# Two-head attention pairs on a padded array against four heads on 64x64 quarters, with the transposes moved to the DMA queue

## The chip, the cores and the metric

The kernel runs on one core of a Trainium2 chip. TensorE (PE) multiplies, VectorE (DVE), ScalarE (ACT) and GpSimd (POOL) work on the results, and DMA queues, most of them driven by SyncE (SP), move data. The metric is the time of one execution on the device in microseconds (us), as the median of a few runs; lower is better.

## The reference

Attention without a softmax, for 8 batches, 12 heads, 448 tokens and 64 values per head, followed by a gated two-layer network over the 3584 tokens:

```python
scores = scale * np.matmul(q, k.transpose(0, 1, 3, 2))     # scale = 1/8
attn = np.maximum(scores, 0.0) ** 2 / S                    # S = 448
x = np.matmul(attn, v)          # the 12 heads side by side: 3584 x 768
h = x @ w_in                                               # 768 x 2048
g = h * (1.0 / (1.0 + np.exp(-1.702 * h)))
out = g @ w_out                                            # 2048 x 768
```

The two constant factors of the attention are left out on the chip and folded into later scales (SC = 64 x 448 = 28672).

## The kernel before

Data arrive as float32, are cast to float16, multiplied, and accumulated in float32 in PSUM.

**Attention.** `attn_pair` handles two heads of one batch. The 448 tokens of a head lie on 112 partitions with four tokens each (`SQ` = 112). Five DMAs on SP's queue bring q, k and v (L64, L66, L69), VectorE casts them, and eight TensorE transposes against an identity (L82) put q and k with the head's 64 values on the partitions, the first head on partitions 0 to 63, the second on 64 to 127; VectorE copies the result to `qkt` (L89). For each of four groups of 112 keys, two matmuls with 64 rows each give the scores of the two heads (`sc`, L96), ScalarE takes the relu (`rl`, L103), VectorE squares it (`attnT`, L104), and two matmuls add to `av` (L106). There the stationary operand `vn` is 128 columns wide and holds v of one head beside 64 columns of zeros (POOL's memset, L71, VectorE's casts, L73), so that both heads' results land in their own half of one accumulator. ScalarE copies `av` to `xt` (L113). There are 48 such pairs.

**First layer.** `moe1_chunk` makes 128 of the 2048 hidden values for one batch of 448 tokens: six matmuls (L128), a sigmoid on ScalarE (L135) and a product on VectorE (L136). There are 16 of them per batch.

**Second layer.** `moe2_chunk` makes 128 tokens of the output from two batches' hidden values: two times 16 matmuls of 384 columns (L151), ScalarE's scaled copy (L157), and output DMAs on SP's queue (L165).

**Order.** Stage 0 is the first batch's attention, followed by the weights: 28 DMAs on SP's queue (L177, L182), each cast by VectorE. In stage 1 to 8, `weave` deals the next batch's attention pairs among the first layer's chunks of the batch before, and in every second stage among seven chunks of the second layer too. The tile framework makes the semaphores and orders each engine's instructions.

## Time and profile before

| what | value |
|---|---|
| time, median of 3 runs | 535.62 us (535.36 to 536.15) |
| span of the profiled execution | 528.7 us (its own time is not listed apart; 6.9 us lie between its span and the median) |
| PE busy (matmul) | 481.4 us, 91% |
| DVE busy | 294.0 us, 56% |
| ACT busy | 281.3 us, 53% |
| POOL busy | 48.3 us, 9% |
| DMA | 57.14 MB moved, mean 108 GB/s |

The span runs from the first to the last instruction of the profiled execution. Busy time counts an engine's own instructions. Matmuls are pipelined and their ends are modelled, so the step from one start to the next says more than a matmul's listed duration.

### The profile page before, as it was taken

The page shows a single profiled execution, that of the slowest core. Times are in us where ns is not written, and L with a number is a line of the kernel's source. Part 1 is how long each engine was busy: PE and PEld are TensorE (multiplying, and loading weights), DVE is VectorE, ACT ScalarE, POOL GpSimd, SP SyncE. Part 2 cuts the span into 40 slices and gives each one's busy share as a digit, 9 for nine tenths or more (in the row PEclk, how much of TensorE's full clock was granted, in tenths as well). Part 3 has the DMA queues.
Part 4 walks back from the last instruction along what each step waited for, and adds up shares of the span by engine and source line. Part 5 has one row for each costly group of instructions (what it writes and reads, how often), then busy time and mean ns, then how long its engine had stood idle before and what let it go on. Part 6 is the DMA issues. An engine that isn't in the chain of part 4 may idle for free.

```text
span 528.7 us, 7760 instructions
## 1 busy us (share of the span) xinstructions
PE 481.4 (91%) x2816; PEld 237.0 (45%) x2816; DVE 294.0 (56%) x589; ACT 281.3 (53%) x426; POOL 48.3 (9%) x54
## 2 busy tenths in 40 slices
PE   1776838789999999999999999999999999999996
PEld 1332413334455554444456554444456554445663
DVE  3686857887730248887740248887740248855000
ACT  2566415776741447776741447776741457764111
POOL 1121001211100001011110000111010000100000
PEclk9889977999999999999999999999999999999999
DMA  6668888563232434443332434443332432000222
GB/s 166 168 227 263 268 256 184 139 147 97 71 102 64 109 95 104 105 100 88 77 100 60 113 94 105 106 102 80 80 100 62 112 96 69 2 1 0 61 71 79
DMA packets 109158, 57.14 MB, mean 108 GB/s; under 512 B 91200, under 2 KB 101952, under 8 KB 109120
## 3 DMA queue, kind: packets, MB, share of 16 engines
q1 hardware_dynamic: 109120, 56.64, 40.6%
q8 instruction: 22, 0.36, 0.3%
q14 instruction: 16, 0.13, 0.1%
HBM read 45.61 MB, written 11.01 MB: 107 GB/s over the span
## 4 chain that ended last, share of the span: by engine, by line
PE 68%; DVE 10%; DMA 9%; ACT 4%; issue 4%; POOL 3%; SPq 2%; DVEq 0%; POOLq 0%; ACTq 0%
PE op L151 26%; PE ht L128 17%; PE av L106 15%; PE sc L96 8%; ACT rl L103 3%; DMA t<-in_moe_w_in_dram 3%; POOL vn L71 3%; DVE qkt L89 2%; DMA t<-in_moe_w_out_dram 2%; PE qkt_ps L82 2%; DVE vn L73 2%; DVE gt L136 2%; DMA kn<-in_k_dram 2%; DMA vs<-in_v_dram 2%; DVE attnT L104 1%
## 5 line engine op out<-in xcount | busy, mean ns | idle before, releaser
L103 ACT ACTIVATE rl<-sc 112x896 f16<-112x896 f32 x192 | 166.1, 921 | 49.2 <-PE sc L96 48.6
L128 PE MATMUL ht<-xt,win 128*128 128x448 f16 x768 | 176.3, 353 | 6.4 <-DVE gt L136 3.5
L151 PE MATMUL op<-wout,gt 128*128 128x384 f16 x896 | 151.8, 326 | 0.0
L104 DVE TENSOR_TENSOR attnT<-rl 112x896 f16<-112x896 f16 x192 | 119.0, 624 | 41.8 <-ACT rl L103 39.0
L106 PE MATMUL av<-attnT,vn 112*128 112x448 f16 x384 | 107.8, 364 | 7.7 <-DVE attnT L104 7.4
L151 PEld LDWEIGHTS <-gt 128*128 128x128 f16 x896 | 86.8, 98 | 60.4 <-issue 3.2
L128 PEld LDWEIGHTS <-win 128*128 128x128 f16 x768 | 70.7, 97 | 82.2 <-issue 22.4
L135 ACT ACTIVATE sg<-ht 128x448 f32<-128x448 f32 x128 | 70.0, 549 | 50.5 <-PE ht L128 46.4
L136 DVE TENSOR_TENSOR gt<-ht,sg 128x448 f16<-128x448 f32 x128 | 79.1, 619 | 19.5 <-ACT sg L135 19.1
L71 POOL MEMSET vn<- 112x1024 f16 x48 | 47.8, 995 | 407.9 <-PE av L106 392.4
L157 ACT ACTIVATE osb<-op 128x384 f32<-128x384 f32 x56 | 27.5, 491 | 105.4 <-PE op L151 105.4
L96 PE MATMUL sc<-qkt 64*112 64x448 f16 x384 | 69.0, 388 | 11.2 <-ACT rl L103 5.6
L76 DVE CAST qnf<-qn 112x512 f16<-112x512 f32 x48 | 24.4, 509 | 96.8 <-PE qkt_ps L82 89.1
L106 PEld LDWEIGHTS <-vn 112*128 112x128 f16 x384 | 33.6, 99 | 47.9 <-issue 35.5
L96 PEld LDWEIGHTS <-qkt 64*112 64x112 f16 x384 | 24.9, 127 | 65.6 <-issue 40.9
L113 ACT ACTIVATE xt<-av 128x448 f16<-128x448 f32 x48 | 26.1, 544 | 37.2 <-PE av L106 35.4
L82 PE MATMUL qkt_ps<-identf,qnf 112*128 112x112 f16 x192 | 20.6, 223 | 16.6 <-DVE identf L53 9.3
L73 DVE CAST vn<-vs 112x256 f16<-112x256 f32 x96 | 23.6, 286 | 20.9 <-POOL vn L71 20.0
L89 DVE COPY qkt<-qkt_ps 128x896 f16<-128x896 f16 x48 | 29.6, 616 | 2.8 <-PE qkt_ps L82 2.8
L82 PEld LDWEIGHTS <-qnf 112*128 112x128 f16 x192 | 16.0, 103 | 28.3 <-DVE qnf L76 13.4
L78 DVE CAST knf<-kn 112x512 f16<-112x512 f32 x48 | 22.5, 470 | 2.1 <-DMA kn<-in_k_dram 2.1
L82 PE MATMUL qkt_ps<-identf,knf 112*128 112x112 f16 x192 | 19.9, 224 | 0.4 <-DVE knf L78 0.4
(12 smaller groups left out, 34.5 us busy)
## 6 DMA issues: line engine op xcount, KB each, us to landing
qn<-in_q_dram SPq DMA_DIRECT2D x96, 112.0 KB, 3.1
kn<-in_k_dram SPq DMA_DIRECT2D x96, 112.0 KB, 3.1
vs<-in_v_dram SPq DMA_DIRECT2D x48, 224.0 KB, 2.9
t<-in_moe_w_in_dram SPq DMA_DIRECT2D x12, 512.0 KB, 4.5
t<-in_moe_w_out_dram SPq DMA_DIRECT2D x16, 384.0 KB, 3.8
out_dram<-osb SPq DMA_DIRECT2D x8, 336.0 KB, 3.1
out_dram<-osb SPq DMA_DIRECT2D x8, 288.0 KB, 2.6
out_dram<-osb SPq DMA_DIRECT2D x8, 240.0 KB, 2.6
```

Source lines behind the costliest of these rows:

```text
L71: nc.gpsimd.memset(vn, 0.0)
L73: nc.vector.tensor_copy(out=vn[:, h, :, h * D:(h + 1) * D], in_=vs[:, h, :, :])
L82: nc.tensor.matmul(out=qkt_ps[:, i, si * SQ:(si + 1) * SQ], lhsT=src[:, si, :, :], rhs=identf[:, :], is_transpose=True,)
L89: nc.vector.tensor_copy(out=qkt, in_=qkt_ps[:, :, 0:S])
L96: nc.tensor.matmul(out=sc[0:SQ, h, 0:S], lhsT=qkt[64 * h:64 * h + 64, 1, t2 * SQ:(t2 + 1) * SQ], rhs=qkt[64 * h:64 * h + 64, 0, 0:S], star ...
L103: nc.scalar.activation(out=rl, in_=sc[0:SQ, :, 0:S], func=AF.Relu)
L104: nc.vector.tensor_tensor(out=attnT[:, t2, :, :], in0=rl, in1=rl, op=ALU.mult)
L106: nc.tensor.matmul(out=av[:, 0:S], lhsT=vn[:, h, t2, :], rhs=attnT[:, t2, h, :], start=(t2 == 0 and h == 0), stop=(t2 == 3 and h == 1),)
L128: nc.tensor.matmul(out=ht[:, 0:S], lhsT=win[:, kk, f * 128:(f + 1) * 128], rhs=xt[:, kk, :], start=(kk == 0), stop=(kk == NK - 1),)
L135: nc.scalar.activation(out=sg, in_=ht[:, 0:S], func=AF.Sigmoid, scale=1.702 / SC)
L136: nc.vector.tensor_tensor(out=gt[:, f, boff:boff + S], in0=ht[:, 0:S], in1=sg, op=ALU.mult)
L151: nc.tensor.matmul(out=op[:, 0:NOUT], lhsT=gt[:, f, jm:jm + 128], rhs=wout[:, f, n * NOUT:(n + 1) * NOUT], start=(f == 0), stop=(f == NF - 1),
```

## The change

- **Heads.** A unit is four heads of one batch: heads 2pr and 2pr+1 on partitions 0 to 63, heads 6+2pr and 7+2pr on 64 to 127. A token index is p*7 + j, with p from 0 to 63 and j from 0 to 6 (`J` = 7). There are 3 units per batch (`NP`), 24 in all (`NU`), and 7 slots (j) in each.
- **Loads.** Six DMAs per unit on SP's queue, each of 64 partitions with two rows of 1792 bytes.
- **Casts and transposes.** VectorE casts q and k, POOL casts v; q and k are then transposed from SBUF to SBUF by `dma_start_transpose` on SP's queue, two transposes per unit, each of 128 x 896 float16 (seven blocks of 128 x 128). TensorE's transposes, the identity and the copy `qkt` are gone, and so are the zero-padded `vn` and its memset.
- **Scores and av.** Per slot four score matmuls of 448 columns, each with 64 rows and 64 stationary columns, on the four quarters of the array; likewise four for `av`. ScalarE's relu and VectorE's square work on 128 x 896.
- **Copy of av.** VectorE copies `av` (128 x 896) to `xt`, in one or two pieces, once per unit.
- **First layer.** Tokens come in eight groups of 384 or 512 in turn (`gblk`). One ScalarE instruction gives the gated value (`Gelu_apprx_sigmoid`); POOL multiplies by SC and casts to float16.
- **Second layer.** VectorE makes the scaled copy; two output DMAs for each 128 tokens.
- **Weights.** Eight DMAs on POOL's queue, four each for `win` and `wout`, which cast from float32 to float16 on the way.
- **Order.** Written by hand (`manual_schedule`). A visit issues the scores of two new slots, the `av` matmuls of the slots before, and then the new slots' relu and square. The first batch's visits come first, then chunks of the two layers (`m1`, `m2`) with a visit after every 3.4 us that the program reckons for them; when a group of tokens needs a batch that is not done, visits are issued one behind the other until it is.

```diff
-    ident = cst.tile([SQ, SQ], F32)
-    make_identity(nc, ident)
...
+    win = [cst.tile([128, NK, WQ * 128], F16, name=f"win{i}") for i in range(NF // WQ)]
+    wout = [cst.tile([128, WQ, DM], F16, name=f"wout{i}") for i in range(NF // WQ)]
...
+    def load(u):
+        b, pr = divmod(u, NP)
+        st = {}
+        for n, t in (("k", k), ("q", q), ("v", v)):
+            x = stp.tile([128, 2, S], F32, name=f"{n}st", tag=f"{n}st")
+            for s in range(2):
+                h0 = 6 * s + 2 * pr
+                nc.sync.dma_start(
+                    out=x[64 * s:64 * s + 64, :, :],
+                    in_=t[b, h0:h0 + 2].rearrange("a (p j) d -> p a (j d)", j=J))
+            st[n] = x
+        units[u] = st
+    def cast(u):
+        st = units[u]
+        for n in ("k", "q"):
+            c = c16.tile([128, J, 2, D], F16, name=f"{n}16", tag=f"{n}16")
+            nc.vector.tensor_copy(
+                out=c.rearrange("p j a d -> p a j d"),
+                in_=st[n].rearrange("p a (j d) -> p a j d", d=D))
+            st[n + "16"] = c
+        vv = v16p.tile([128, 2, J, D], F16, name="v16", tag="v16")
+        nc.gpsimd.tensor_copy(out=vv, in_=st["v"].rearrange("p a (j d) -> p a j d", d=D))
+        st["v16"] = vv
+    def trans(u):
+        st = units[u]
+        for n in ("k", "q"):
+            t = qkT.tile([128, J, 128], F16, name=f"{n}T", tag=f"{n}T")
+            nc.sync.dma_start_transpose(
+                out=t[:, :, :], in_=st[n + "16"].rearrange("p j a d -> p (j a d)"))
+            st[n + "T"] = t
+    def scores(u, j):
+        st = units[u]
+        sc = ps_s.tile([128, 2, 512], F32, name="sc", tag="sc")
+        for s in range(2):
+            for a in range(2):
+                r = slice(64 * a, 64 * a + 64)
+                c = slice(64 * s, 64 * s + 64)
+                nc.tensor.matmul(
+                    out=sc[c, a, 0:S],
+                    lhsT=st["kT"][r, j, c],
+                    rhs=st["qT"][r, :, c],
+                    start=True, stop=True)
+        return sc
+    def relu2(u, j, sc):
+        rl = rlp.tile([128, 2, S], F16, name="rl", tag="rl")
+        nc.scalar.activation(out=rl, in_=sc[:, :, 0:S], func=AF.Relu)
+        at = atp.tile([128, 2, S], F16, name="at", tag="at")
+        nc.vector.tensor_tensor(out=at, in0=rl, in1=rl, op=ALU.mult)
+        return at
+    def av_mm(u, j, at):
+        st = units[u]
+        if j == 0:
+            st["av"] = ps_v.tile([128, 2, 512], F32, name="av", tag="av")
+        for s in range(2):
+            for a in range(2):
+                r = slice(64 * s, 64 * s + 64)
+                nc.tensor.matmul(
+                    out=st["av"][64 * a:64 * a + 64, s, 0:S],
+                    lhsT=st["v16"][r, a, j, :],
+                    rhs=at[r, a, :],
+                    start=(j == 0), stop=(j == J - 1))
+    def xt_evac(u):
+        b, pr = divmod(u, NP)
+        av = units[u]["av"]
+        lo = b * J
+        while lo < (b + 1) * J:
+            g = max(i for i in range(NG) if gcum[i] <= lo)
+            hi = min((b + 1) * J, gcum[g + 1])
+            if g not in xts:
+                xts[g] = xtp.tile([128, 2, NP, 512], F16, name="xt", tag="xt")
+            nc.vector.tensor_copy(
+                out=xts[g][:, :, pr, 64 * (lo - gcum[g]):64 * (hi - gcum[g])],
+                in_=av[:, :, 64 * (lo - b * J):64 * (hi - b * J)])
+            lo = hi
+        units[u] = None
+    slots = [(u, j) for u in range(NU) for j in range(J)]
+    pend = []
+    pos = [0]
+    done_units = [0]
+    def visit(n):
+        new = slots[pos[0]:pos[0] + n]
+        pos[0] += len(new)
+        scs = [scores(u, j) for u, j in new]
+        ready = []
+        while pend:
+            ready.append(pend.pop(0))
+            if ready[-1][1] == J - 1:
+                break
+        for u, j, at in ready:
+            av_mm(u, j, at)
+        if ready and ready[-1][1] == J - 1:
+            xt_evac(ready[-1][0])
+            done_units[0] = ready[-1][0] + 1
+        for (u, j), sc in zip(new, scs):
+            pend.append((u, j, relu2(u, j, sc)))
...
-        sg = mo.tile([128, S], F32, tag="sg")
-        nc.scalar.activation(out=sg, in_=ht[:, 0:S], func=AF.Sigmoid, scale=1.702 / SC)
-        nc.vector.tensor_tensor(out=gt[:, f, boff:boff + S], in0=ht[:, 0:S], in1=sg,
-                                op=ALU.mult)
...
+                out=ht[:, 0:n], lhsT=w[:, kk, fo:fo + 128],
+                rhs=xts[g][:, kk // NP, kk % NP, 0:n],
+                start=(kk == 0), stop=(kk == NK - 1))
+        gf = gfp.tile([128, 512], F32, name="gf", tag="gf")
+        nc.scalar.activation(out=gf[:, 0:n], in_=ht[:, 0:n],
+                             func=AF.Gelu_apprx_sigmoid, scale=1.0 / SC)
+        nc.gpsimd.tensor_scalar(out=gts[g][:, f, 0:n], in0=gf[:, 0:n],
+                                scalar1=SC, scalar2=1.0, op0=ALU.mult, op1=ALU.mult)
+    osb = {}
+    def m2(g, m, h):
+        if h == 0:
+            osb[g, m] = osp.tile([128, DM], F32, name="osb", tag="osb")
+        ot = osb[g, m]
+        op = ps_m.tile([128, 512], F32, name="op", tag="mm")
+        for f in range(NF):
+            nc.tensor.matmul(
+                out=op[:, 0:NOUT],
+                lhsT=gts[g][:, f, m * 128:(m + 1) * 128],
+                rhs=wout[f // WQ][:, f % WQ, h * NOUT:(h + 1) * NOUT],
+                start=(f == 0), stop=(f == NF - 1))
+        nc.vector.tensor_scalar(out=ot[:, h * NOUT:(h + 1) * NOUT], in0=op[:, 0:NOUT],
+                                scalar1=1.0 / SC, scalar2=None, op0=ALU.mult)
+        if h == 1:
+            for i in range(2):
+                b, j = divmod(gcum[g] + 2 * m + i, J)
+                r0 = b * S + j
+                nc.sync.dma_start(out=out[r0:r0 + 63 * J + 1:J, :],
+                                  in_=ot[64 * i:64 * i + 64, :])
+    def w1(i):
+        nc.gpsimd.dma_start(
+            out=win[i],
+            in_=moe_w_in[:, i * WQ * 128:(i + 1) * WQ * 128].rearrange(
+                "(kk p) f -> p kk f", p=128))
+    def w2(i):
+        nc.gpsimd.dma_start(
+            out=wout[i],
+            in_=moe_w_out[i * WQ * 128:(i + 1) * WQ * 128, :].rearrange(
+                "(f p) d -> p f d", p=128))
+    def t1(g):
+        return 6 * (64 * gblk[g] / 2400.0 + 0.0025)
+    T2 = 16 * (NOUT / 2400.0 + 0.0025)
+    for ph in range(1, NG + 2):
+        a = [("m1", ph - 1, f) for f in range(NF)] if ph - 1 < NG else []
+        c = ([("m2", ph - 2, m, h) for m in range(gblk[ph - 2] // 2) for h in range(2)]
+             if ph >= 2 else [])
+        if a and c:
+            seq = []
+            ci = 0
+            for i, x in enumerate(a):
+                seq.append(x)
+                while ci < len(c) and (i + 1) * len(c) >= (ci + 1) * len(a):
+                    seq.append(c[ci])
+                    ci += 1
+            seq += c[ci:]
         else:
+            seq = a + c
+        moe += seq
+    with tc.manual_schedule():
+        loaded = [0]
+        prepped = [0]
+        def prefetch(upto_load, upto_prep):
+            while loaded[0] < min(NU, upto_load):
+                load(loaded[0])
+                loaded[0] += 1
+            while prepped[0] < min(NU, upto_prep):
+                cast(prepped[0])
+                trans(prepped[0])
+                prepped[0] += 1
+        prefetch(2, 0)
+        prefetch(2, 1)
+        prefetch(3, 2)
+        prefetch(3, 3)
+        for i in range(NF // WQ):
+            w1(i)
+        prefetch(6, 3)
+        for i in range(NF // WQ):
+            w2(i)
+        def step_visit(n):
+            u = slots[pos[0]][0]
+            prefetch(u + 4, u + 2)
+            visit(n)
+        while done_units[0] < NP:
+            if pos[0] < NP * J:
+                step_visit(min(2, NP * J - pos[0]))
+            else:
+                visit(0)
+        acc = 0.0
+        TV = 3.4
+        m1_done = 0
+        for it in moe:
+            if it[0] == "m1":
+                g = it[1]
+                need = NP * min(B, -(-gcum[g + 1] // J))
+                while done_units[0] < need:
+                    if pos[0] < len(slots):
+                        step_visit(2)
+                    else:
+                        visit(0)
+                m1(*it[1:])
+                acc += t1(g)
+            else:
+                m2(*it[1:])
+                acc += T2
+            if it[0] == "m1" and it[2] == NF - 1:
+                m1_done = it[1] + 1
+            if acc >= TV and (pos[0] < len(slots) or pend):
+                if pos[0] < len(slots):
+                    if slots[min(pos[0] + 1, len(slots) - 1)][0] // NP + 1 - 3 < m1_done:
+                        step_visit(2)
+                else:
+                    visit(0)
+                acc -= TV
```

## Rows read from the trace of the kernel before

**Rows 1.** The page's first lines: span, then each engine's busy time, share and instructions.

```profile
span 528.7 us, 7760 instructions
PE 481.4 (91%) x2816; PEld 237.0 (45%) x2816; DVE 294.0 (56%) x589; ACT 281.3 (53%) x426; POOL 48.3 (9%) x54
```

**Rows 2.** Busy time by stretch: length, busy us per engine, granted clock, DMA share, GB/s.

```profile
40.00:50.00 10.00, 6.95 (x41) 2.95 (x40) 8.02 (x15) 5.33 (x7) 0.95 (x1) 1.00 0.77 258
50.00:60.00 10.00, 7.07 (x37) 3.44 (x37) 7.26 (x13) 5.53 (x10) 1.20 (x1) 1.00 0.90 261
60.00:70.00 10.00, 8.80 (x46) 4.27 (x45) 7.25 (x15) 4.34 (x8) 0.00 (x0) 1.00 0.83 274
70.00:80.00 10.00, 1.83 (x12) 0.82 (x10) 5.59 (x13) 0.56 (x2) 0.00 (x0) 0.63 0.93 249
...
160.00:200.00 40.00, 39.77 (x250) 21.45 (x247) 12.23 (x26) 15.69 (x27) 1.90 (x2) 1.00 0.35 93
```

**Rows 3.** The chain that ended last, its final pieces: start us, us, what.

```profile
469.78 17.63 PE ht L128 x93
487.41 36.41 PE op L151 x224
```

**Rows 4.** Groups by line: shapes, count, busy us, mean ns, idle before.

```profile
L103 ACT ACTIVATE rl<-sc 112x896 f16<-112x896 f32 x192 | 166.1, 921 | 49.2 <-PE sc L96 48.6 <-DVE attnT L104 0.4 <-DVE qnf L76 0.2
L104 DVE TENSOR_TENSOR attnT<-rl 112x896 f16<-112x896 f16 x192 | 119.0, 624 | 41.8 <-ACT rl L103 39.0
L106 PE MATMUL av<-attnT,vn 112*128 112x448 f16 x384 | 107.8, 364 | 7.7 <-DVE attnT L104 7.4
L136 DVE TENSOR_TENSOR gt<-ht,sg 128x448 f16<-128x448 f32 x128 | 79.1, 619 | 19.5 <-ACT sg L135 19.1
L135 ACT ACTIVATE sg<-ht 128x448 f32<-128x448 f32 x128 | 70.0, 549 | 50.5 <-PE ht L128 46.4 <-DVE gt L136 4.1
L96 PE MATMUL sc<-qkt 64*112 64x448 f16 x384 | 69.0, 388 | 11.2 <-ACT rl L103 5.6 <-DVE qkt L89 4.0
L71 POOL MEMSET vn<- 112x1024 f16 x48 | 47.8, 995 | 407.9 <-PE av L106 392.4 <-DVE qkt L89 15.4
L157 ACT ACTIVATE osb<-op 128x384 f32<-128x384 f32 x56 | 27.5, 491 | 105.4 <-PE op L151 105.4
L82 PE MATMUL qkt_ps<-identf,qnf 112*128 112x112 f16 x192 | 20.6, 223 | 16.6 <-DVE identf L53 9.3 <-DVE qnf L76 7.4
```

**Rows 5.** Timeline of PE in the last attention stage: start us, us, instruction.

```profile
450.22 0.59 PE L96 MATMUL sc<-qkt 64*112 64x448 f16 x4
450.74 0.93 PE L128 MATMUL ht<-xt,win 128*128 128x448 f16 x4
451.63 0.40 PE L96 MATMUL sc<-qkt 64*112 64x448 f16 x2
451.96 0.36 PE L128 MATMUL ht<-xt,win 128*128 128x448 f16 x1
...
453.10 0.54 PE L106 MATMUL av<-attnT,vn 112*128 112x448 f16 x2
453.48 0.54 PE L128 MATMUL ht<-xt,win 128*128 128x448 f16 x2
...
455.90 0.36 PE L82 MATMUL qkt_ps<-identf,qnf 112*128 112x112 f16 x4
456.10 0.36 PE L82 MATMUL qkt_ps<-identf,knf 112*128 112x112 f16 x4
```

**Rows 6.** DMA issues on SP's queue by source: duration of the issue, then time to landing.

```profile
L69 SPq DMA_DIRECT2D vs<-in_v_dram x48: 318/340/614, 3.5 to 444.6; - x48
...
DMA to landing us min/median/max: 2.5/2.9/4.6
...
L165 SPq DMA_DIRECT2D out_dram<-osb x56: 314/412/589, 154.9 to 524.7; - x56
```

**Rows 7.** Timeline of the start: the first load's cast on VectorE.

```profile
5.08 0.43 DVE L76 CAST qnf<-qn 112x512 f16<-112x512 f32 x1 [5.08 <-DMA qn<-in_q_dram]
```

More of the change, by code (lines that the diff above doesn't have):

```diff
@@ L6 @@
 from concourse import bass_utils, mybir
-from concourse.masks import make_identity
 from concourse._compat import with_exitstack
@@ L36 @@
     SC = float(D * S)
-    cst = ctx.enter_context(tc.tile_pool(name="cst", bufs=1))
+    WQ = 4
+    gblk = [6, 8] * (B // 2)
+    gcum = [0]
+    for n in gblk:
+        gcum.append(gcum[-1] + n)
+    NG = len(gblk)
+    cst = ctx.enter_context(tc.tile_pool(name="cst", bufs=1))
+    stp = ctx.enter_context(tc.tile_pool(name="stp", bufs=3))
+    c16 = ctx.enter_context(tc.tile_pool(name="c16", bufs=2))
+    v16p = ctx.enter_context(tc.tile_pool(name="v16p", bufs=4))
+    qkT = ctx.enter_context(tc.tile_pool(name="qkT", bufs=3))
@@ L115, in attn_chunks @@
-    def attn_chunks(b):
-        xt = xtp.tile([128, NK, S], F16, name="xt", tag="xt")
-        xts[b] = xt
-        return [lambda hp=hp: attn_pair(b, hp) for hp in range(NHP)]
-    gts = {}
-    def moe1_chunk(b, f):
-        xt = xts[b]
-        gt = gts[b // 2]
-        boff = (b % 2) * S
-        ht = ps_m.tile([128, 512], F32, tag="mps")
+    osp = ctx.enter_context(tc.tile_pool(name="osp", bufs=3))
+    ps_s = ctx.enter_context(tc.tile_pool(name="ps_s", bufs=2, space=bass.MemoryType.PSUM))
@@ new lines @@
+    ps_v = ctx.enter_context(tc.tile_pool(name="ps_v", bufs=1, space=bass.MemoryType.PSUM))
+    ps_m = ctx.enter_context(tc.tile_pool(name="ps_m", bufs=2, space=bass.MemoryType.PSUM))
+    win = [cst.tile([128, NK, WQ * 128], F16, name=f"win{i}") for i in range(NF // WQ)]
+    wout = [cst.tile([128, WQ, DM], F16, name=f"wout{i}") for i in range(NF // WQ)]
+    units = {}
+    def load(u):
[10 more added lines that the diff above has]
+        units[u] = st
@@ L127, in moe1_chunk, with m1 @@
+    gts = {}
+    def m1(g, f):
+        n = 64 * gblk[g]
+        if f == 0:
+            gts[g] = gtp.tile([128, NF, 512], F16, name="gt", tag="gt")
+        ht = ps_m.tile([128, 512], F32, name="ht", tag="mm")
+        w = win[f // WQ]
+        fo = (f % WQ) * 128
         for kk in range(NK):
             nc.tensor.matmul(
-                out=ht[:, 0:S],
-                lhsT=win[:, kk, f * 128:(f + 1) * 128],
-                rhs=xt[:, kk, :],
-                start=(kk == 0), stop=(kk == NK - 1),
-            )
@@ L171, in moe2_chunks @@
-    def moe2_chunks(pair):
-        return [lambda m=m: moe2_chunk(pair, m) for m in range(2 * S // 128)]
-    def weight_chunks():
-        def w1(kk, hf):
-            t = tmp.tile([128, DFF // 2], F32, tag="wtmp")
-            nc.sync.dma_start(out=t, in_=moe_w_in[kk * 128:(kk + 1) * 128,
-                                                  hf * DFF // 2:(hf + 1) * DFF // 2])
-            nc.vector.tensor_copy(out=win[:, kk, hf * DFF // 2:(hf + 1) * DFF // 2], in_=t)
-        def w2(f):
-            t = tmp.tile([128, DM], F32, tag="wtmp")
-            nc.sync.dma_start(out=t, in_=moe_w_out[f * 128:(f + 1) * 128, :])
-            nc.vector.tensor_copy(out=wout[:, f, :], in_=t)
-        return ([lambda kk=kk, hf=hf: w1(kk, hf) for kk in range(NK) for hf in range(2)]
-                + [lambda f=f: w2(f) for f in range(NF)])
@@ L187, in weave @@
-    def weave(at, mc):
-        seq = []
-        ai = 0
-        for j, c in enumerate(mc):
-            while ai < len(at) and ai * len(mc) <= j * len(at):
-                seq.append(at[ai])
-                ai += 1
-            seq.append(c)
-        seq.extend(at[ai:])
-        return seq
-    for st in range(B + 1):
-        at = attn_chunks(st) if st < B else []
-        if st == 0:
-            seq = at + weight_chunks()
-        else:
-            mc = moe1_chunks(st - 1)
-            if st >= 2 and st % 2 == 0:
-                mc = mc + moe2_chunks(st // 2 - 1)
-            seq = weave(at, mc)
-        for c in seq:
-            c()
+                out=ht[:, 0:n], lhsT=w[:, kk, fo:fo + 128],
@@ new lines, in w1 @@
+    def w1(i):
[8 more added lines that the diff above has]
+                "(f p) d -> p f d", p=128))
+    moe = []
+    def t1(g):
+        return 6 * (64 * gblk[g] / 2400.0 + 0.0025)
+    T2 = 16 * (NOUT / 2400.0 + 0.0025)
```

102 lines of the change are left out of this document (6 added, 96 removed).

## The prediction

> **What bounds the kernel now.** I read the page's first lines, then the busy time by stretch, then the chain that ended last, then single instructions. PE is busy for 481.4 of 528.7 us, and no other engine for more than 294.0 [rows 1]. The stretches show two regimes. From stage 2 on PE is the limit: 39.77 of 40 us are busy at the full granted clock while the DMA engines are busy for a third [rows 2]. Up to about 80 us it is not: PE is busy for 7 to 9 of 10 us, and for 1.83 between 70 and 80 us, while the DMA engines are busy for 77 to 93% at 249 to 274 GB/s, 260 on average [rows 2]: there the weights and the next batch's heads arrive. So the change is worth what it takes off PE after the start, less what it adds to a start that DMA sets.
>
> **The two layers, which stay.** At the end 93 matmuls of 448 columns take 17.63 us, 0.190 each, and 224 of 384 columns take 36.41, 0.1625 each [rows 3]; between them lie 0.42 ns per column, so 512 columns take 0.217. The first layer has 768 matmuls, half of 384 columns and half of 512: 62.4 + 83.2 = 145.6 us. The second has 896 of 384: 145.6. Together 291.2, the same as before.
>
> **What leaves PE.** Scores are busy for 69.0 us, av for 107.8, transposes for 20.6 with q and about as much with k [rows 4]: some 218 us.
>
> **What replaces it.** A visit holds 8 score and 8 av matmuls of 448 columns on quarters. Two score matmuls on different rows (L96 x2) start at 451.63 and the next line at 451.96: 0.33 us for 0.19 of streaming, so they ran together and 0.14 went with the change from half rows to full [rows 5]. L96 x4 takes 0.52, two times 0.19 and 0.14. Four full matmuls in front of scores take 0.89, 0.13 over 0.76, and two av matmuls, which use the full array now, lead into other full ones after 0.38, nothing over [rows 5]. A visit is one block of quarters with one change in and one out, 0.27. If the four quarters run together it is 4 x 0.19 + 0.27 = 1.03; a weight load and its short matmul take 0.05 (four transposes from 455.90 to 456.10 [rows 5]), and 16 of those give 0.8 + 0.27 = 1.07. No row shows matmuls side by side in the columns: with two at a time the visit is 8 x 0.19 + 0.27 = 1.79, one at a time 3.3. I take 1.05, nearest to the rows that overlap already.
>
> Written out, the program has 12 visits in the first batch, 64 paced ones and a last one (4 of the paced in the first phase of the layers), and 10 issued one behind the other (8 of them at the second phase's start). Where nothing lies between visits, ScalarE sets the pace: two relus at 0.92 [rows 4], 1.84 a visit.
>
> **Engines that become no bound.** ScalarE: 168 relus at 0.92 and 128 gated values at 0.55: 225 us. VectorE: 168 squares at 0.62, 48 casts of 896 at 0.75 (0.43 for 512 [rows 7]), 24 copies of av at 1.24 (0.62 for 448 from PSUM), 56 output copies at 0.49 [rows 4]: 198 us. POOL: its memset does 1024 elements in 0.995 [rows 4], so 128 products of up to 512 and 24 casts of 896 are 86 us; a product would have to take 1.3 us, a first-layer chunk's PE time, to matter. All are priced at nothing under some 410 us of PE; should that cover be gone, each one's sum above is its cost. The gated value's second pass on VectorE (L136) and the memset go, also at no gain, since they are hidden now.
>
> **DMA and its queue.** SP issues six loads per unit; one like them costs it 0.34 us and lands after 2.9, an output DMA 0.41 [rows 6]. 144 loads and 56 outputs are 72 us. A transpose has no row. Below, it is a load of the same bytes, 0.34 us of queue; above, its seven blocks follow each other, each landing before the next, 7 x 2.9 = 20.3. I take 1 to 3 us, as one instruction of 229 KB with the bytes of a load: at 3 us SP's sum is 216 us, under PE. Behind a transpose, which waits for VectorE's cast, stand the later loads and outputs; three units of loads lie ahead, so these wait without PE. The Trainium skill (VectorE: DVE Perf Modes, The three transpose paths) gives 390 ns for a 128x128 transpose on TensorE and 1309 ns on the DMA crossbar. Seven of those in a row would be an estimated 9.2 us per transpose, and the sum would then be the fifth case's below instead of mine; no run here shows it.
>
> **The sum.** First scores: the first load is there at 5.08 us [rows 7], two casts make 6.6, two transposes with a landing of 2.9 about 10, and the 2.75 MB of two units take 10.6 us at 260 GB/s: I take 12 (10 to 14). First batch: 21 x 0.92 = 19.3, and 1.5 for its last square, av and copy: 32.8. First phase: 96 x 0.1625 = 15.6 and 4 x 1.05: 52.6. Eight visits at ScalarE's pace, 14.7: 67.3. Three chunks of 1.3 and a visit, then the first second-layer chunk: 72.3. It needs all of `wout`.
>
> Here stands the one new wait that I count. By then the queues have been given nine units (12.4 MB), both weights (12.6 MB read) and 2.75 MB of transposes: 27.7 MB, 107 us at 260 GB/s. The weights' last piece comes somewhat before the last unit: 100. Bounds: 85, as 274 GB/s came at a share of 0.83 [rows 2] and full use would be 330; and 148, if a casting DMA counts double for 12.6 MB. No DMA left POOL's queue before, so nothing shows its price. PE takes its instructions in order and waits 27.7 us; the forced visits' loads are late for the same reason, which is in the same 100. After it: 275.6 of the layers from the second phase on, 2 x 1.84 and 61 x 1.05: 343.4, less the 5.0 already counted. The end: 2 for the last chunk's gated value and product, and 4.9 from the last matmul to the end of the span, as now (523.8 to 528.7 [rows 1, 3]). 100 + 338.4 + 6.9 = 445.3 us of span. The median lies 6.9 above the span before (535.62 to 528.7), so 452.
>
> **The rivals.** Second: the weights are there sooner and the wait shrinks or goes, 424 to 437 us; for it, 3 KB and 2 KB rows in place of 256-byte ones, against it, 93% busy engines at 249 GB/s [rows 2]. Third: weights from POOL's queue are slow, doubled by the cast or late because POOL makes them behind its own work; `wout` at 148, 500 us. POOL's v casts and products stand behind these eight DMAs, so a blocked POOL holds the first layer's PSUM through ScalarE as well. The Trainium skill (SBUF — State Buffer, Who interferes with whom) says that VectorE's two-port casts lock POOL out while it writes descriptors; no row of before can show that. Fourth: only two quarters run together: 0.74 x 61 = 45 us more, 497. Fifth, the slower side: the transposes fill SP's queue. From the first transpose at 5 us to the last unit, then some 62 us of layers without attention and 5 at the end: 5 + 72 + 48 T + 67 passes 528.7 from T = 8.0 us on. At T = 10, 624 us of span, 631. For it, that the crossing lies inside the bounds of 0.34 and 20.3; against it, 229 KB that as a load occupy the queue for 0.34.
>
> **How the numbers follow.** The forecast case (437 to 470 us, 452 as its point) 0.47, earlier weights 0.10, slow weights 0.15, half-parallel quarters 0.14, transposes as the bound 0.14, of which 0.02 for a time within 0.2% of now. Runs of this kernel lie 0.15% apart, so 0.2% is about what can be told from no change. Faster is 0.47 + 0.10 + 0.15 + 0.14 = 0.86, slower 0.12. The range reaches from 418, under the second case's end by a first score at 10 us and visits at 1.0, to 510, over the third and fourth; it leaves out the fifth and what two mishaps together give.
>
> **What would show it.** Right: PE near 40 of 40 us from the second phase on; a visit of 16 quarter matmuls from first start to the next full one in about 1.05 us; PE's idle time before the first `op` matmul ended by the DMA into `wout` near 100 us; ScalarE without gaps in the first batch's relus; issues of transposes on SP under 3 us. Wrong: score matmuls released by transposes all along (fifth), visits near 1.8 (fourth), the first `op` after 130 us (third) or POOL's products pacing the first layer.

## The result, and the profile after

The changed kernel takes 461.49 us (median of 4 runs, 460.75 to 463.11), the kernel before 535.49 in the same comparison. The ratio on record is 0.865, 95% interval 0.8605 to 0.8695 (the two medians alone give 0.862, inside it). 452 was forecast. The profiled execution took 461.49 us itself, with a span of 459.7.

The page's head and two of its queues, after (answering to [rows 1]); a queue's line has packets, MB, and the share of 16 engines over the span:

```profile
span 459.7 us, 7621 instructions
PE 391.4 (85%) x3008; PEld 196.2 (43%) x3008; DVE 192.6 (42%) x308; ACT 212.0 (46%) x298; POOL 107.4 (23%) x164
...
q1 hardware_dynamic: 69760, 55.07, 54.9%
q0 software_dynamic: 5248, 6.29, 8.1%
```

PE is still the busiest engine, but its share fell from 91% to 85%: it lost 90.0 us of work, and the span only 69.0. PE's idle time rose from 47.3 to 68.3 us, and 54.4 of it lie before 120 us (65.6 us busy until then). Busy time by stretch, after, columns as in [rows 2]:

```profile
40.00:50.00 10.00, 7.68 (x44) 3.27 (x39) 4.19 (x7) 4.91 (x8) 1.73 (x5) 0.80 1.16 271
50.00:60.00 10.00, 0.00 (x0) 0.00 (x0) 0.00 (x0) 0.00 (x0) 1.35 (x2) 0.71 1.22 212
60.00:70.00 10.00, 0.00 (x0) 0.00 (x0) 0.00 (x0) 0.00 (x0) 0.00 (x0) 0.50 1.17 203
70.00:80.00 10.00, 9.07 (x59) 4.40 (x60) 2.50 (x4) 5.80 (x9) 2.14 (x5) 0.77 1.25 242
80.00:90.00 10.00, 9.24 (x87) 4.60 (x85) 4.41 (x7) 7.71 (x13) 4.71 (x9) 1.00 0.69 149
90.00:100.00 10.00, 6.71 (x64) 2.74 (x67) 8.88 (x13) 6.99 (x9) 2.76 (x3) 0.59 0.94 187
...
160.00:200.00 40.00, 40.00 (x339) 21.37 (x336) 20.02 (x32) 22.81 (x34) 11.15 (x17) 1.00 0.67 141
...
280.00:320.00 40.00, 37.50 (x307) 18.54 (x306) 20.77 (x33) 21.42 (x30) 9.91 (x15) 1.00 0.73 150
```

From 50 to 70 us no compute engine but POOL does anything, while the DMA share is above 1, which I read as engines that are full. The TensorE clock granted falls to 0.50 there, after PE has stood still. From 160 to 440 us PE is busy for 37.50 to 40.00 of each 40 us, at the full granted clock. PE's instructions in order of time, after (start, duration, and in brackets the idle time before the first of them and who ended it; [rows 5] is its counterpart):

```profile
16.83 0.96 PE L106 MATMUL sc<-qT,kT 64*64 64x448 f16 x8 [16.83 <-DMA qT<-q]
...
22.35 1.13 PE L127 MATMUL av<-at,v 64*64 64x448 f16 x8 [2.52 <-DVE at L117]
...
37.68 1.03 PE L127 MATMUL av<-at,v 64*64 64x448 f16 x8 [2.91 <-DVE at L117]
...
42.69 0.50 PE L183 MATMUL ht<-xt,win 128*128 128x384 f16 x2
43.82 5.41 PE L183 MATMUL ht<-xt,win 128*128 128x384 f16 x22 [0.63 <-DVE xt L144]
...
70.93 0.96 PE L106 MATMUL sc<-qT,kT 64*64 64x448 f16 x8 [21.69 <-DMA qT<-q]
...
88.09 0.57 PE L106 MATMUL sc<-qT,kT 64*64 64x448 f16 x8
...
105.36 0.61 PE L183 MATMUL ht<-xt,win 128*128 128x512 f16 x2
...
111.82 2.76 PE L201 MATMUL op<-wout,gt 128*128 128x384 f16 x16
114.51 0.57 PE L106 MATMUL sc<-qT,kT 64*64 64x448 f16 x8
114.91 0.55 PE L127 MATMUL av<-at,v 64*64 64x448 f16 x8
115.39 2.76 PE L183 MATMUL ht<-xt,win 128*128 128x512 f16 x12
...
127.43 2.77 PE L201 MATMUL op<-wout,gt 128*128 128x384 f16 x16
130.04 1.46 PE L183 MATMUL ht<-xt,win 128*128 128x512 f16 x6
```

Two readings. The 21.69 us end with a transpose into `qT` (unit 3), not with `wout`. And a visit takes 0.40 + 0.48 us from the first quarter matmul to the next full one; the full chunk ahead of it takes 2.69 (111.82 to 114.51) where it leads into quarters and 2.61 (127.43 to 130.04) where it does not. So a visit costs 0.96: eight scores and eight `av` in four groups of about 0.19, and 0.2 for the two changes of tile.

SP's queue in the start and around the standstill, after (start, the queue's time for the instruction or instructions), and what the trace says of `wout` (issue times in ns and us, then landing):

```profile
7.42 1.25 SPq L73 DMA_DIRECT2D vst<-in_v_dram  x2
8.79 1.34 SPq L95 DMA_TRANSPOSE kT<-k  x1
...
46.20 1.23 SPq L95 DMA_TRANSPOSE kT<-k  x1
47.53 10.58 SPq L95 DMA_TRANSPOSE qT<-q  x1
...
64.86 9.36 SPq L95 DMA_TRANSPOSE kT<-k  x1
```

```profile
L222 POOL DMA_DIRECT2D wout<-in_moe_w_out_dram x4: 785/790/800, 27.6 to 29.8; - x4
...
DMA to landing us min/median/max: 33.9/39.5/47.0
```

All of `wout` is there by 29.8 + 47.0 = 76.8 us, 35 us before its first use. Of the three transposes around the standstill the first holds SP's queue for 1.23 us, near the median of 1.25, and the next two for 10.58 and 9.36; the DMA share is above 1 under all three.

### The profile page after: what moved, and what is told of

Its sections match the earlier page's. It is cut to its first block, busy times and chain, and to the rows that moved or that the text cites. A ratio compares the mean times of both kernels' runs of the same rounds, so it can differ in the third digit from the quotient of the medians.

```text
span 459.7 us, 7621 instructions
## 1 busy us (share of the span) xinstructions
PE 391.4 (85%) x3008; PEld 196.2 (43%) x3008; DVE 192.6 (42%) x308; ACT 212.0 (46%) x298; POOL 107.4 (23%) x164
## 3 DMA queue, kind: packets, MB, share of 16 engines
q1 hardware_dynamic: 69760, 55.07, 54.9%
q0 software_dynamic: 5248, 6.29, 8.1%
## 4 chain that ended last, share of the span: by engine, by line
PE 74%; DMA 12%; DVE 8%; SPq 3%; issue 2%; ACT 1%; DVEq 0%; ACTq 0%
PE op L201 31%; PE ht L183 31%; PE sc L106 6%; DMA qT<-q 6%; PE av L127 5%; DMA qst<-in_q_dram 3%; DVE xt L144 3%; DMA kst<-in_k_dram 2%; DVE at L117 2%; SPq L73 2%; DVE k L83 1%; DVE q L83 1%; ACT rl L115 1%; SPq L95 1%; DVE osb L206 0%
## 5 line engine op out<-in xcount | busy, mean ns | idle before, releaser
L115 ACT ACTIVATE rl<-sc 128x896 f16<-128x896 f32 x168 | 144.5, 917 | 121.5 <-PE sc L106 113.7
L183 PE MATMUL ht<-xt,win 128*128 128x384 f16 (+1 forms) x768 | 161.6, 358 | 8.3 <-DVE xt L144 8.3
L117 DVE TENSOR_TENSOR at<-rl 128x896 f16<-128x896 f16 x168 | 107.6, 655 | 106.8 <-ACT rl L115 106.6
L190 POOL TENSOR_SCALAR gt<-gf 128x384 f16<-128x384 f32 (+1 forms) x128 | 77.3, 604 | 295.0 <-ACT gf L188 292.8
L188 ACT ACTIVATE gf<-ht 128x384 f32<-128x384 f32 (+1 forms) x128 | 69.8, 545 | 98.0 <-PE ht L183 82.6
L106 PE MATMUL sc<-qT,kT 64*64 64x448 f16 x672 | 56.0, 393 | 45.1 <-DMA qT<-q 40.0
L206 DVE TENSOR_SCALAR osb<-op 128x384 f32<-128x384 f32 x56 | 31.2, 557 | 132.7 <-PE op L201 131.9
L127 PE MATMUL av<-at,v 64*64 64x448 f16 x672 | 54.1, 381 | 10.2 <-DVE at L117 9.7
L88 POOL CAST v<-vst 128x896 f16<-128x896 f32 x24 | 23.4, 981 | 30.3 <-DMA vst<-in_v_dram 29.2
L144 DVE CAST xt<-av 128x768 f16<-128x768 f32 (+2 forms) x36 | 26.8, 772 | 3.8 <-PE av L127 3.7
```

The lines of the kernel that those rows point to most:

```text
L88: nc.gpsimd.tensor_copy(out=vv, in_=st["v"].rearrange("p a (j d) -> p a j d", d=D))
L106: nc.tensor.matmul(out=sc[c, a, 0:S], lhsT=st["kT"][r, j, c], rhs=st["qT"][r, :, c], start=True, stop=True)
L115: nc.scalar.activation(out=rl, in_=sc[:, :, 0:S], func=AF.Relu)
L117: nc.vector.tensor_tensor(out=at, in0=rl, in1=rl, op=ALU.mult)
L127: nc.tensor.matmul(out=st["av"][64 * a:64 * a + 64, s, 0:S], lhsT=st["v16"][r, a, j, :], rhs=at[r, a, :], start=(j == 0), stop=(j == J - 1))
L144: nc.vector.tensor_copy(out=xts[g][:, :, pr, 64 * (lo - gcum[g]):64 * (hi - gcum[g])], in_=av[:, :, 64 * (lo - b * J):64 * (hi - b * J)])
```

## The experiments

Each ratio is to the kernel before, timed in the same comparison. "First second-layer chunk" is the start of PE's first `op` matmul.

| kernel | time, us | ratio, 95% interval | first second-layer chunk, us |
|---|---|---|---|
| the change | 461.49 | 0.865 [0.8605, 0.8695] | 111.8 |
| `wout` later | 464.95 | 0.872 [0.8667, 0.8772] | 114.7 |
| a quarter of the weights | 442.08 | 0.8289 [0.8246, 0.8331] | 93.3 |
| one transpose per unit | 448.99 | 0.8418 [0.8372, 0.8465] | 99.5 |
| `av` on halves | 485.72 | 0.9109 [0.9061, 0.9157] | 111.4 |
| six units transposed on TensorE | 451.67 | 0.8462 [0.8425, 0.8498] | 103.9 |
| all units on TensorE, in line | 510.82 | 0.9565 [0.9538, 0.9593] | 106.1 |
| transposes ahead of loads | 463.28 | 0.8682 [0.8659, 0.8705] | 114.9 |
| gate in two passes | 477.18 | 0.8937 [0.8912, 0.8961] | 115.9 |
| start reworked | 442.14 | 0.8274 [0.8245, 0.8303] | 93.5 |
| all units on TensorE, cast ahead | 470.58 | 0.8804 [0.8778, 0.883] | 99.1 |
| kernel before, gate in one pass | 532.82 | 0.9981 [0.9957, 1.0005] | |
| start reworked, a quarter of the weights | 435.98 | 0.8181 [0.815, 0.8211] | 86.3 |

**`wout` later.** Is the standstill a matter of order, in that `wout` crowds out unit 3's transposes?

```diff
-        for i in range(NF // WQ):
-            w2(i)
...
+            if prepped[0] >= 6 and not w2_done[0]:
+                w2_done[0] = 1
+                for i in range(NF // WQ):
+                    w2(i)
```

> Edit: the four DMAs of wout are issued on POOL's queue only when unit 5's transposes have been issued, in place of right behind win. Theory A (the weights crowd the DMA engines, and unit 3's transposes wait behind them from 48 to 71 us): that wait of 21.7 us falls below 8, wout lands near 95 to 100 us, the first second-layer chunk starts near 100 in place of 112, time 448 to 453 us. Theory B (the transposes themselves fill the DMA engines, at some 3 us of all 16 engines each, so that the order of the issues matters little): first second-layer chunk at 108 to 112, time 457 to 462.

PE's timeline and the busy time by stretch of this kernel:

```profile
58.05 0.96 PE L106 MATMUL sc<-qT,kT 64*64 64x448 f16 x8 [11.16 <-DMA qT<-q]
...
103.65 0.59 PE L106 MATMUL sc<-qT,kT 64*64 64x448 f16 x4 [13.39 <-DMA qT<-q]
```

```profile
90.00:100.00 10.00, 0.26 (x4) 0.00 (x0) 1.53 (x3) 1.24 (x2) 0.00 (x0) 0.50 1.16 221
```

Unit 3's wait shrank from 21.69 to 11.16 us, and another one of 13.39 us came, from 90 to 104 us, after `wout` had been issued from 77.3 us on. The wait moved; the time did not fall. The time lies 3 us past theory B's band, and theory A's gain did not come. Order alone is not the cause.

**A quarter of the weights.** Takes six of the eight weight transfers away and leaves every instruction that computes.

```diff
-        w = win[f // WQ]
+        w = win[0]
...
-        for i in range(NF // WQ):
-            w1(i)
+        w1(0)
```

(`wout` likewise.)

> Edit: only the first quarter of each weight matrix is loaded and used for all four quarters (the result is that of other weights). 9.4 MB of reads leave the start. Theory A (weights crowd the engines): no wait of PE for a transpose over 5 us after the first batch, first second-layer chunk at 72 to 78 us, time 422 to 430. Theory B (transposes fill the engines): first second-layer chunk at 85 to 95 us, time 437 to 447.

```profile
52.40 0.57 PE L106 MATMUL sc<-qT,kT 64*64 64x448 f16 x8 [3.65 <-DMA qT<-q]
...
93.32 2.76 PE L201 MATMUL op<-wout,gt 128*128 128x384 f16 x16
```

PE's timeline has 3.65 us left of the 21.69, the first second-layer chunk comes 18.5 us sooner and the time is 19.4 us shorter: what the start gains is still there at the end. Chunk and time lie in theory B's bands, the shrunken wait is what theory A had said; the next experiment tests theory B's price.

**One transpose per unit.** What does a transpose cost the DMA engines?

```diff
-        for n in ("k", "q"):
+        for n in ("k",):
...
+        st["qT"] = st["kT"]
```

> Edit: only k is transposed, and k's transpose stands for q's in the scores (the result is that of q = k). 24 of 48 transposes go, with 5.5 MB of 61.8 moved. Theory A (weights crowd the engines): the remaining transpose of unit 3 still waits behind the weights, 12 to 22 us, time 452 to 458. Theory B (a transpose costs some 3 us of all engines): 9 of 18 transposes ahead of the first second-layer chunk are 27 us less of DMA, first second-layer chunk at 85 to 92 us, time 433 to 442.

The queue's line of this kernel's page (span 446.1 us):

```profile
q1 hardware_dynamic: 47488, 49.56, 48.8%
```

24 transposes fewer are 22272 packets fewer, 928 each, and the queue's time falls from 54.9% of 459.7 us (252.4) to 48.8% of 446.1 (217.7): 34.7 / 24 = 1.45 us of all sixteen engines for each. That is one pair of runs, and the queue's time differs by itself: the six runs with the change's packets on this queue have 238.6 to 252.4 us. The two kernels below that use no DMA transpose have 176.8 and 177.3, which puts a transpose at 1.3 to 1.6. The time lies between the two forecasts: a transpose is dearer than its bytes, and half of the 3 us that the second theory had given it. From here on the theory (C) is the sum of all DMA work in the start, not one kind of it.

**`av` on halves.** Is a group of four quarters really one pass? `v` is padded with zeros to 128 columns, so that two `av` matmuls run at a time instead of four.

```diff
-        for s in range(2):
-            for a in range(2):
+        for a in range(2):
+            for s in range(2):
...
-                    out=st["av"][64 * a:64 * a + 64, s, 0:S],
+                    out=st["av"][:, s, 0:S],
```

> Edit: av's stationary operand is 128 columns wide with zeros beside the head's 64 values, as in the kernel before, so its four matmuls per slot run on half-arrays of 64 rows, two at a time, and not on quarters; POOL casts v in two pieces. If the quarters run four wide, av of a visit goes from 0.38 to 0.76 us, and the 63 visits that PE paces add 24 us, with more at each change of shape: 484 to 495. If the columns do not run side by side (two matmuls at a time already now), no change: 460 to 464.

```profile
163.16 0.93 PE L133 MATMUL av<-at,vpad 64*128 64x448 f16 x8
164.03 2.12 PE L189 MATMUL ht<-xt,win 128*128 128x384 f16 x12
```

In PE's timeline the eight `av` take 0.87 us up to the next full matmul, 0.48 before, and the time grows by 24.2 us. The four quarters do run side by side.

**Six units transposed on TensorE.** The first six units' transposes leave the DMA queue (fourteen TensorE transposes per unit into a score buffer, copied by VectorE for k and ScalarE for q); the weights are issued somewhat later, between the first batch's visits.

```diff
-                trans(prepped[0])
+                (trans_pe if prepped[0] < 6 else trans)(prepped[0])
```

> Edit: q and k of the first six units (two batches) are transposed on TensorE into a score buffer in PSUM and copied out by VectorE (k) and ScalarE (q); from unit 6 on the DMA transposes stay. win is issued at the fourth visit, wout when unit 3 has been cast. Theory C (up to the first second-layer chunk the sum of all DMA work sets the time; a transpose is 1.45 us of all 16 engines, as 24 of them took 555 engine-us): 12 transposes less are 17 us, and the first scores come 3 us sooner, without the transposes' landing: first second-layer chunk at 92 to 97 us in place of 112, time 441 to 447. Theory D (the weights and loads alone saturate the engines until then): 107 to 111, 456 to 461.

```profile
78.42 0.93 PE L101 MATMUL tp<-ident,k 128*128 128x128 f16 x7 [4.55 <-DVE k L88]
```

9.8 us faster than the change, and in between both forecasts. PE's timeline shows one reason why not more: the transposes stand in PE's order right behind their cast, and PE waits for it (10.9 us in four waits for k's cast). The later weights and the missing transposes were not tried apart.

**All units on TensorE, in line.**

```diff
-                trans(prepped[0])
+                trans_pe(prepped[0])
```

> Edit: all 24 units are transposed on TensorE as in the run above, no DMA transposes at all. Per unit PE gets 14 transposes at some 0.055 us and a change of shape, 0.9 us; for the 18 units behind the start that is 16 us on the engine that sets the time there. Theory C: 457 to 463, that is 14 to 18 above the run with six units. If the DMA transposes cost PE waits behind the start too, that difference is smaller: 447 to 455.

510.82 us was in neither forecast. PE's timeline and a stretch well past the start:

```profile
215.88 0.56 PE L101 MATMUL tp<-ident,k 128*128 128x128 f16 x7 [0.59 <-DVE k L88]
...
218.65 0.38 PE L130 MATMUL sc<-qT,kT 64*64 64x448 f16 x4 [1.35 <-ACT qT L112]
```

```profile
200.00:240.00 40.00, 33.51 (x282) 15.98 (x280) 18.69 (x32) 21.01 (x28) 7.61 (x12) 0.96 0.42 103
```

PE is busy for 33.51 of 40 us where the change has 38.44: it stands for the cast (11.6 us behind 120 us) and for the copy that gives back the score buffer which the transposes borrow (21.6 us). The forecasts had counted the transposes' own time alone.

**Transposes ahead of loads.** Is it the order on SP's queue, the transposes standing behind loads that nobody needs yet?

```diff
-            while prepped[0] < min(NU, upto_prep):
+            while prepped[0] < min(loaded[0], upto_prep):
...
+            while loaded[0] < min(NU, upto_load):
+                load(loaded[0])
+                loaded[0] += 1
```

> Edit: on SP's queue a unit's two transposes stand ahead of the next unit's six loads in place of behind them (at the start unit 2's loads still stand behind unit 0's transposes). Six loads are 3.7 us of the queue. Theory C (sum of DMA work): the order changes little, first second-layer chunk at 108 to 113, time 457 to 463. Theory E (the chain cast, queue, transpose, landing of one unit sets the pace of the start, some 11 us against 6.5 of work per unit when visits follow each other): 3.7 us less for each of units 3 to 6, first second-layer chunk at 98 to 102, 447 to 452.

```profile
70.49 0.96 PE L106 MATMUL sc<-qT,kT 64*64 64x448 f16 x8 [23.14 <-DMA qT<-q]
```

463.28 us, and the wait for unit 3 was 23.14 in PE's timeline: no gain, as theory C had said (its bands are missed by 0.3 us and, for the chunk, by 1.9). The order on SP's queue is not the cause.

**Gate in two passes.** The old gate in the new kernel.

```diff
-                             func=AF.Gelu_apprx_sigmoid, scale=1.0 / SC)
-        nc.gpsimd.tensor_scalar(out=gts[g][:, f, 0:n], in0=gf[:, 0:n],
-                                scalar1=SC, scalar2=1.0, op0=ALU.mult, op1=ALU.mult)
+                             func=AF.Sigmoid, scale=1.702 / SC)
+        nc.vector.tensor_tensor(out=gts[g][:, f, 0:n], in0=ht[:, 0:n], in1=gf[:, 0:n],
+                                op=ALU.mult)
```

> Edit: the one-pass gate is undone: ScalarE gives the sigmoid, VectorE multiplies it with the hidden values from PSUM into gt, and POOL's product goes. VectorE gets 128 times 0.62 = 79 us more, on 193 of 460 busy now. The prediction's step (all of this is hidden under PE): no change, 460 to 463. Rival (PSUM is held longer, two buffers for both layers, so PE waits): each first-layer chunk behind a visit waits up to 0.6 us, 466 to 475.

15.7 us slower than the change, just past the rival's band; 4 us of it up to the first second-layer chunk, 11.6 behind it. PE's waits behind 120 us (total, times, longest) have a line that the change lacks, and from 120 to 280 us PE is busy for 152.2 us, 155.4 in the change (one of the four stretches and one of the waits in PE's timeline are shown):

```profile
PE op L201 <- DVE gt L190: 5.9, 13, 1.5
```

```profile
200.00:240.00 40.00, 37.55 (x307) 17.51 (x305) 25.84 (x43) 22.68 (x32) 2.62 (x3) 1.00 0.70 147
```

```profile
177.01 2.12 PE L183 MATMUL ht<-xt,win 128*128 128x384 f16 x12
180.64 2.76 PE L201 MATMUL op<-wout,gt 128*128 128x384 f16 x16 [1.50 <-DVE gt L190]
```

So the gate in one pass is worth 15.7 us here, with VectorE far from full (25.84 of 40 us). All 13 waits have the form shown: twelve `ht` matmuls, which are two tiles and fill both PSUM buffers of the layers (`ps_m`), and then an `op`, which reads an earlier group's `gt` and so can only be waiting for a buffer. VectorE's product of the first `ht` gives it back; in one pass ScalarE gives it back. These waits are 5.9 of the 11.6 us; what makes up the rest is not shown.

**The kernel before, gate in one pass.** The same edit alone, in the kernel before.

> The kernel before, with the one-pass gate alone: ScalarE gives the gated value, POOL multiplies by SC into gt, VectorE's product goes. If the 15.7 us that the changed kernel lost without it come from its two buffers in PSUM, held through both passes: here three buffers serve, PE waits little for them, and the time falls by less than 5 us (530 to 535). If they come from VectorE as the engine behind the squares: VectorE is busier here, and the time falls by 10 or more (515 to 525).

0.9981, no change that can be told, as the first forecast had it. The gate's worth depends on the kernel around it. PE's waits for the product are 3.5 us in the kernel before, all four of them between 54 and 70 us, where DMA sets the pace [rows 2]. What differs near the gate is the number of PSUM buffers for `ht` (three before, two after) and VectorE's queue, which in the change also has the copies of `av` (1.08 us for 128 x 896 in the mean). The trace above shows that PE waits for a buffer; whether a third buffer alone would bring the 15.7 us back was not tried.

**Start reworked.** The six units on TensorE, cast one unit ahead and issued behind a visit; their k cast on POOL; the weights issued as the casts get on; a visit every 1.5 us in the first phase.

```diff
+            if prepped[0] > 2 and not issued[0]:
+                issued[0] = 1
+                for i in range(NF // WQ):
+                    w1(i)
...
+            if j >= 2:
+                turn(u + 2)
...
+            tv = 1.5 if m1_done == 0 else TV
```

> Edit: as in the run with six units transposed on TensorE, but a unit is cast a visit or more ahead (k of these units on POOL) and transposed behind a visit's matmuls, so that PE does not stand before the cast; win is issued when unit 2 has been cast, wout when unit 4 has; in the first phase of the layers a visit follows every 1.5 us of chunks in place of 3.4, so that the second batch is done by its end and no block of visits stands alone. Theory C (sum of the DMA work: units 0 to 5 8.3 MB, weights 12.6 MB read, at the rates of the runs so far done near 75 us): first second-layer chunk at 76 to 84 us, time 425 to 434. Rival (the start is paced by ScalarE and by loads in a chain, whatever the transposes do): 95 to 104, 443 to 452.

442.14 us: faster than both kernels, 19.4 us under the change. PE's timeline has the first second-layer chunk at 93.51, 1.5 us short of the rival's band; the sum of DMA work alone had promised 76 to 84. Five things are changed together here, and their shares were not tried apart.

```profile
93.51 2.76 PE L225 MATMUL op<-wout,gt 128*128 128x384 f16 x16
```

**All units on TensorE, cast ahead.** The same rework for all 24 units (a visit every 3.4 us).

> Edit: all 24 units transposed on TensorE in that way (cast ahead, transposes behind a visit), the visits of the first phase after 3.4 us as in the changed kernel. Theory F (the earlier run without DMA transposes lost its 59 us to PE standing in line for the cast, the copy and a score buffer, not to the transposes' 0.9 us per unit): 455 to 470. Rival (the extra changes of shape and the third user of two score buffers cost 2.5 us per unit however they stand): 495 to 510.

470.58 us, 0.6 past theory F's band: casting ahead gives back 40 of the 49 us that the version in line had lost. Its first second-layer chunk comes at 99.1 us, 13 sooner than in the change, and it ends 9 us later: past the start, transposes on PE cost more than on the DMA queue, for which the change's PE waits 1.1 us behind 111 us.

**Start reworked, a quarter of the weights.** What holds the reworked start?

> The reworked start once more, with only the first quarter of each weight loaded and used for all four (so all four quarters of the hidden values are computed from the first quarter of the weights; the number and shape of all instructions on the five engines stay). It asks what sets the reworked start, whose first second-layer chunk came at 93.5 us and whose time was 442.14 us. Theory C, the sum of all DMA work until then: the six weight transfers left out are three quarters of the 37 us that the eight take of all sixteen engines, 28 us; in the changed kernel the same step moved the first second-layer chunk by 18.5 us and the time by 19.4 us. If DMA still sets the start, the first second-layer chunk comes between 72 and 84 us and the time is 420 to 433 us. Rival, the chain of casts, transposes, copies, relus and squares over VectorE and ScalarE, with PE at half its clock for part of it: the chunk stays between 89 and 95 us and the time between 437 and 444 us. Between the two bands both hold a part.

Busy time by stretch and PE's timeline of this kernel:

```profile
40.00:60.00 20.00, 18.07 (x149) 8.20 (x145) 10.48 (x16) 14.11 (x21) 8.19 (x12) 0.84 0.68 158
60.00:80.00 20.00, 16.68 (x171) 7.79 (x170) 14.65 (x21) 15.73 (x24) 8.98 (x12) 1.00 0.68 162
```

```profile
86.27 2.76 PE L225 MATMUL op<-wout,gt 128*128 128x384 f16 x16
```

7.2 us of the 18.5 that the same step gave in the change. The chunk lies about midway between the two bands, the time (435.98) nearer to the rival's: both hold a part, DMA some 7 us of it. With the DMA share at 0.68 the chunk still comes at 86.3, so full engines no longer set it. That the chain of casts, copies, relus and squares does is argued: followed back from there, the chain that ends last is 28.4 us PE's own work, 20.9 VectorE's, 15.7 ScalarE's and 8.8 DMA landings, and no one step was taken out to test it.

## Why the prediction held, and where it did not

**Held: what PE sheds, and the regime past the start.** From the first second-layer chunk to the end of the span, 338.4 + 6.9 = 345.3 us were forecast and 347.9 measured. A visit measured 0.96 where 1.05 was taken (5.5 us less over 61), and PE waits for 9.0 us there that the sum lacks, 6.4 of them for the copy into `xt` (total, times, longest):

```profile
PE ht L183 <- DVE xt L144: 6.4, 5, 1.6
```

The errors cancel in part, so the sum is nearer than its terms. The changes of tile cost 0.2 per visit, forecast 0.27. The rival of half-parallel quarters fell, and `av` on halves shows its price for `av` alone, 24.2 us.

**Held: the engines that are no bound.** ScalarE 212.0 us (225 forecast), VectorE 192.6 (198), POOL 107.4 (86). POOL's product takes 0.604 us, under the 1.3 from which it would matter. That they cost nothing held under PE, past the start, and not in the start (below).

**Held: the fifth case's test.** A transpose holds SP's queue for 1.25 us in the median, within the 1 to 3 taken and far from 8.0. The prediction had worked out an estimate of 9.2 us from the 1309 ns that the Trainium skill (VectorE: DVE Perf Modes, The three transpose paths) gives for one block; for seven blocks in one instruction the trace does not agree, with 1.25 us of queue and 4.4 to 4.7 from issue to landing. But SP's loads were underpriced: 0.61 to 0.65 us each where 0.34 was taken. The third case fell too: POOL had issued the last weight by 30.6 us, and the casting DMAs took 37 us of all engines, 11 less than their 12.6 MB at 260 GB/s. The second case's argument had compared rows of different tensors: in the kernel before the 256-byte rows were the heads', and the weights came in rows of 4 and 3 KB.

**Half right: the one new wait.** That full DMA engines make PE stand for some 28 us in the start was the argument; PE stood for 21.69 in one piece and more in small ones. That it would stand at `wout` was wrong: `wout` was there at 76.8 us, and what came late were unit 3's transposes, for which PE stood from 49.2 us on. The step that failed is the pricing of the transposes by their bytes at a load's rate, and with it the place of the wait.

The sum of all engines' time until the first second-layer chunk, by the measured prices: ten units of loads (13.8 MB) at 249 GB/s, which is what the queue moved in the kernel without DMA transposes (44.05 MB in 37.7% of 469.1 us), are 55 us; both weights 8.1% of 459.7, 37; the sixteen transposes issued by then at 1.45, 23: together 115 us, and the chunk came at 111.8. The forecast's 107 has 48 for nine units' loads, 48 for the weights and 10.6 for transposes; its 2.75 MB are only twelve of them, six units', which by the measured price are 17. Errors of opposite sign, the weights too dear, the transposes too cheap and too few, gave nearly the right sum and the wrong place, which is luck. The measured sum is no proof either: from 80 to 90 us the DMA share was 0.69, so the engines were not full all the way to the chunk. The quarter of the weights and the single transpose test the sum from two sides: 28 and 12 us less work, 18.5 and 12.3 us sooner. Why the first falls 9 us short of its 28 is not shown; a second limit beside DMA, like the one of the last experiment, would fit.

**Wrong in size: the start ahead of the wait.** First scores at 16.83 us (12 forecast, 10 to 14): twelve loads at over 0.6 us each keep SP's queue until 8.67, so the first transpose goes out at 8.79, and the scores start 6.6 us after the second one's issue at 10.23, where 2.9 was taken for a landing. The first `ht` matmul came at 42.69 us (32.8). Of these 9.9 us, 4.8 are the first scores', and PE's two waits for squares, 2.52 and 2.91, are about the rest: the squares stand in VectorE's order behind casts of a later unit, which wait for that unit's loads. One such cast:

```profile
19.05 0.63 DVE L83 CAST k<-kst 128x896 f16<-128x896 f32 x1 [5.03 <-DMA kst<-in_k_dram]
```

So ScalarE did not run without gaps, as it should have by the prediction's own sign (it is busy for 13.65 us from 20 to 40 us). The forced visits took 17.3 us (14.7):

```profile
88.10:105.40 17.30, 12.82 (x126) 5.39 (x126) 14.56 (x21) 13.26 (x16) 4.22 (x5) 0.61 0.91 182
```

VectorE is the busiest engine there, not ScalarE, and the granted clock is 0.61. These and the place of the wait make the first second-layer chunk 11.8 us late, and with the 2.6 behind it the span 14.4 us longer than forecast.

**Wrong in size, the other way: what lies around the span.** 6.9 us were taken, the median before less a span from another execution; the profiled execution after has 461.49 - 459.7 = 1.8, and every run with both numbers on record, of the kernel before too, has 1.7 to 2.0. These 5.1 us hide a third of the span's error: 459.7 + 1.8 = 461.5 against 445.3 + 6.9 = 452.

**Wrong: the gate "at no gain".** It was priced at nothing because VectorE's pass was hidden before. In the kernel before it was (0.9981), but in the changed one it is worth 15.7 us. VectorE's 294.0 us busy of 528.7 [rows 1] said that there is room, and nothing of when the results are wanted: with the gate in two passes the changed kernel's PE waits 13 times for a PSUM buffer that VectorE's product still holds.

**Open.** What makes up the gate's 15.7 us beyond the 5.9 of PE's waits for a buffer, and whether a third buffer would bring them back; and what in the chain of the reworked start sets its 86 us.

## What to carry to other kernels

Price a transfer by the time that it takes of all DMA engines, measured from a queue's share, and add these up to the first point at which the program needs them all. In this start that sum came near the measured time, and moving transfers about only moved the wait; but look at the share stretch by stretch, since once the engines have room another chain sets the pace. Work moved off the limiting engine can be cheaper past the start and dearer in it, so choose the engine by stage: the best version here transposes six units on TensorE and eighteen on the DMA queue. And undo each small edit by itself on the changed kernel: the gate's pass was free in one kernel and worth 3% in the other.

## What the hardware showed that was not expected

- A DMA transpose of 128 x 896 float16 took 1.45 us of all sixteen engines by one pair of runs, 1.3 to 1.6 by the others, in 928 packets, though it holds only 229 KB (158 GB/s at 1.45); with full engines its issue held SP's queue for up to 10.58 us.
- Weights cast by the DMA on the way took 37 us of all engines for 12.6 MB read (6.29 MB written), less than a plain load's rate of 249 GB/s would give (51): the cast does not double the cost.
- Four 64x64 matmuls of 448 columns ran side by side in 0.19 us, and the change between full and quarter tiles cost about 0.1 us each way.
- In the second half of PE's standstill the granted clock was 0.50 (1.2 GHz); with `wout` later, after PE's wait to 103.65, it still read 0.50 from 100 to 110 us, where PE was busy for 5.54 us.
